# The greatest logit by a diagonal matmul and VectorE in place of GpSimd, and slots written as int32 at once

## The chip, the core and the metric

The kernel runs on one core of a Trainium2 chip. The core has five engines with queues of their own: TensorE (PE; its weight loads are shown as PEld), VectorE (DVE), ScalarE (ACT), GpSimd (POOL) and SyncE (SP, which here only issues transfers). They meet through semaphores. The metric is the device time of one execution in microseconds, as the median of several runs. The median before is 712.11 us, of three runs from 708.58 to 715.13.

## The reference

Eight sequences of 576 tokens go through an attention of eight heads with 64 columns each. Four heads see a local band of 32 keys, four see every 32nd key. The result, 4608 tokens by 512, goes through a mixture of eight experts with a capacity of 576 tokens each. Which expert takes which token is decided greedily over all pairs of token and expert:

```python
cap = N // E
logits = x @ w_gate
order = np.argsort(-logits.flatten())
for idx in order:                       # greatest logit first
    tok, e = (int(idx) // E, int(idx) % E)
    if assigned[tok] >= 0 or counts[e] >= cap:
        continue
    assigned[tok] = e
    counts[e] += 1
...
for e in range(E):
    mask = assigned == e
    h = np.maximum(x[mask] @ w1[e], 0.0)
    out[mask] = h @ w2[e]
```

## The kernel before, in words

**Attention and logits.** The first part runs over the eight sequences and the two kinds of heads, writes the tokens to device memory (`x_scr`, float16 in a high and a low part) and leaves the logits in `L`, 128 partitions by 36 columns by 8 experts: token 128c + p is partition p of column c. As columns are completed, VectorE keeps per partition the greatest absolute logit (`peak`, L521) and per token the greatest logit, its expert and a one-hot of it (`rm0`, `wm0`, `oh0`, by `point`, L192 to L196).

**The first expert's search.** The greedy rule is carried out expert by expert. The one whose capacity fills first is found by bisection over the logit at which it fills. The bisection needs a range that is the same on all partitions: `pk` (L715) is the greatest of `peak` per partition, `rng` (L717) the greatest of these over all partitions, present in each of them, and L718 keeps its power of two. L722 scales a constant grid of thresholds by it. `search0` (L768) then takes six rounds. In each, VectorE compares all tokens with 32 thresholds (`cm`, L778), TensorE counts per threshold and expert (L782), VectorE tests the counts against the capacity (L794), TensorE spreads the result over the partitions (L799), and VectorE forms the next thresholds (L802). The last round gives the expert, whose number `ei` (L887) lets SyncE fetch its weights (L987).

**Slots and indices.** `slots` (L890) numbers the expert's tokens by a prefix sum. `slot` (L918) holds 36 numbers per partition, from 0 to 575 for tokens taken and 8192 and more for others. `take` (L931) reads it to remove the tokens taken from the logits. `indices` (L937) turns it into a list of tokens: `si` splits a slot into its upper part (by 6 bits) and its lower 6 bits (L941 to L943), `sh` is the same in float16 (L945), one-hots of both parts (L947, L955, L949) go through a matmul (L963), and `idx` (L975) is the list. With it GpSimd's queue gathers the tokens (`xg`, L1072). The first expert's tokens are turned by TensorE (L1060), the others' by transposing transfers (L1075).

**Experts.** Each of the eight phases runs the two matrix products of one expert (L1159; L1207 and, for the last half tile, L1201), whose float32 weights are split on the chip into float16 high and low parts (L1020, L1021). Beside the matmuls of one phase run the search for the next expert (`search`, L816, comparison in L824, count in L840), its slots and indices, and the preparation of its weights.

**What sets the order.** TensorE's queue is written out by hand: a small planner in the kernel (due times in `chains`, a clock advanced by the cost of each matmul, L1259 to L1263) inserts the steps of the search among the matmuls; in the first phase ScalarE's queue is written out as well. The other engines' queues after the first search are ordered by the tile framework's list scheduler from its own cost estimates and the priorities of `urgent` (L744), so that one instruction less can exchange its neighbours. Semaphore waits follow from data and from buffers coming free. `rt` keeps two buffers of each name, `ps_r` two PSUM banks for all tiles named `pr_`.

Of the kernel before, what the change touches and what calls it, by code (L numbers as in the profile page):

```python
# [8 lines left out]
F32 = mybir.dt.float32  # L9
F16 = mybir.dt.float16  # L10
BF16 = mybir.dt.bfloat16
I32 = mybir.dt.int32
AF = mybir.ActivationFunctionType
OP = mybir.AluOpType
AX = mybir.AxisListType
# [25 lines left out]
TP = 128  # L41
NC = N // TP
DC, FC = DM // 128, FF // 128
NT = (CAP + 127) // 128
SLO = 64
# [87 lines left out]
def band_stride_attention_then_capacity_moe(ctx, tc, qt, kl, ks, nl, ns, wg, w1, w2, cst, out, dbg=None):  # L133
    nc = tc.nc
# [10 lines left out]
    ident = load_const("ident", [128, 128], F32)  # L145
# [30 lines left out]
    ones_f = const.tile([128, 128], F32, name="ones_f")  # L176
# [526 lines left out]
    rt = ctx.enter_context(tc.tile_pool(name="rt", bufs=2))  # L703
# [5 lines left out]
    ps_r = ctx.enter_context(tc.tile_pool(name="ps_r", bufs=2, space=PSUM))  # L709
# [4 lines left out]
    pk = rt.tile([128, 1], F32, name="pk")  # L714
    nc.vector.tensor_reduce(pk, peak, axis=AX.X, op=OP.max)  # L715
    rng = rt.tile([128, 1], F32, name="rng")
    nc.gpsimd.partition_all_reduce(rng, pk, 128, bass.bass_isa.ReduceOp.max)  # L717
    nc.vector.tensor_single_scalar(rng.bitcast(I32), rng.bitcast(I32), EXPM, op=OP.bitwise_and)  # L718
    grid = r1.tile([128, R0, J0 + 1], F32, name="grid")

# [169 lines left out]
    def slots(ph, rm, ohc, wmc, code, mv):  # L890
# [15 lines left out]
        with urgent(ph):  # L906
            pp = ps_r.tile([128, 512], F32, name="pr_")
            for j in range(2):
                nc.tensor.matmul(pp[:TP, j * 2 * NC:(j + 1) * 2 * NC], tri[:, j * TP:(j + 1) * TP], scf,
                                 start=(j == 0), stop=(j == 1), skip_group_check=True)  # L910
            off = rt.tile([TP, 2 * NC], F32, name="off")
            nc.vector.tensor_scalar(off, scf, -8192.0, 8192.0, op0=OP.mult, op1=OP.add)
            nc.vector.tensor_tensor_scan(inc[:, 1:], ones_f[:TP, :2 * NC], pp[:TP, 2 * NC:4 * NC], 0.0, op0=OP.mult,
                                         op1=OP.add)
            nc.vector.tensor_tensor(off, off, pp[:TP, :2 * NC], op=OP.add)
            nc.vector.tensor_tensor(off, off, inc[:, :2 * NC], op=OP.add)
            slot = rt.tile([TP, NC], F32, name="slot")
            nc.vector.tensor_tensor(slot, off[:, :NC], off[:, NC:], op=OP.min)  # L918
        return slot

# [16 lines left out]
    def indices(ph, slot):  # L937
        hurry = ph in HURRY
        with urgent(ph) if hurry else nullcontext():
            si = rt.tile([TP, 2, NC], I32, name="si")  # L940
            nc.vector.tensor_copy(si[:, 0], slot)  # L941
            nc.vector.tensor_single_scalar(si[:, 1], si[:, 0], SLO - 1, op=OP.bitwise_and)
            nc.vector.tensor_single_scalar(si[:, 0], si[:, 0], 6, op=OP.logical_shift_right)  # L943
            sh = rt.tile([TP, 2, NC], F16, name="sh")
            nc.vector.tensor_copy(sh, si)  # L945
            ohh = rt.tile([TP, SHI, NC], F16, name="ohh")
            nc.vector.tensor_tensor(ohh, sh[:, 0:1].to_broadcast([TP, SHI, NC]), iota[:, :SHI], op=OP.is_equal)  # L947
            rv = rvb[ph % 2]
            nc.vector.tensor_tensor(rv[:, :3 * SHI].rearrange("p (h a) c -> p h a c", a=3), ohh[:, :, None].to_broadcast([TP, SHI, 3, NC]),  # L949
                                    val[:, None].to_broadcast([TP, SHI, 3, NC]), op=OP.mult)  # L950
            nh = NC // 3
            ohl = []
            for h in range(3):
                o = r1.tile([TP, SLO, nh], F16, name=f"ohl{h}")
                nc.vector.tensor_tensor(o, sh[:, 1:2, h * nh:h * nh + nh].to_broadcast([TP, SLO, nh]),  # L955
                                        iota[:, :, :nh], op=OP.is_equal)
                ohl.append(o)
# [373 lines left out]
```

## Time and profile before

| | us |
|---|---|
| median of the runs | 712.11 (708.58 to 715.13) |
| profiled execution, its time | 713.84 |
| its span, first to last instruction | 712.1 |
| TensorE busy | 614.3 (86%) |
| VectorE busy | 465.3 (65%) |
| ScalarE busy | 318.9 (45%) |
| GpSimd busy | 156.7 (22%) |
| mean granted TensorE clock | 0.907 |

The profile is of one execution. Times in its rows are microseconds from the start of the span. A timeline row gives start, length, engine, line and instruction, output and inputs, and in brackets how long the engine had been idle and which event ended that. "issue" stands where no such event is seen. Rows that the profile merges carry a count (x16). The granted clock is the share of its full clock that TensorE was given. Attention ends near 220 us, the search of the first expert goes to about 243 us, the first expert's matmuls begin near 259 us, and the last transfer is issued after 701 us.

### The profile page before, as it was taken

The numbers are of one execution on the slowest core, as the hardware profiler recorded it, in microseconds if no ns is written. First come the engines' busy times: TensorE is split into PE (matmuls) and PEld (weight loads), VectorE is DVE, ScalarE is ACT, GpSimd is POOL, SyncE is SP. The second block draws the span as 40 slices with busy tenths as digits, with TensorE's granted clock in tenths as the row PEclk, the third lists the DMA queues.
The fourth block names the chain that finished last, engine by engine and source line by source line (L and its number), as shares of the span: only waits on it lengthen the run. The fifth ranks groups of instructions, "written<-read, shape, count | busy, mean of one in ns | idle before, by whom it ended". The sixth has DMA issues, their size and how long they took to land.

```text
span 712.1 us, 19031 instructions
## 1 busy us (share of the span) xinstructions
PE 614.3 (86%) x7974; PEld 392.3 (55%) x7977; DVE 465.3 (65%) x1326; ACT 318.9 (45%) x497; POOL 156.7 (22%) x152
## 2 busy tenths in 40 slices
PE   7778777788984368899989999999999989999993
PEld 4555555566663346546635745745654754755741
DVE  4797656787786788858857877867768543552200
ACT  3635634554521055555544644833823746452210
POOL 2053413323331030050041031211212111402011
PEclk9888978987786579999999999999999999999997
DMA  9999999999642270391671671852652684341010
GB/s 252 265 262 255 248 230 255 239 234 209 167 103 67 68 231 28 135 267 36 237 156 45 238 154 46 276 110 90 229 112 75 237 236 151 90 94 52 2 37 29
DMA packets 111472, 111.24 MB, mean 156 GB/s; under 512 B 76405, under 2 KB 84175, under 8 KB 110876
## 3 DMA queue, kind: packets, MB, share of 16 engines
q1 hardware_dynamic: 103307, 88.49, 47.9%
q0 software_dynamic: 7360, 21.15, 9.5%
q8 instruction: 62, 1.02, 0.6%
q10 hardware_dynamic: 720, 0.39, 0.2%
q14 instruction: 23, 0.18, 0.1%
HBM read 73.63 MB, written 18.87 MB: 130 GB/s over the span
## 4 chain that ended last, share of the span: by engine, by line
PE 26%; issue 12%; DVE 10%; DMA 8%; ACT 3%; POOL 2%; SPq 1%; POOLq 0%; ACTq 0%
PE ph L1207 12%; PE ph L1159 8%; DMA w<-in_w_dram 7%; PE ph L1201 2%; DVE w2l L1021 2%; ACT jk L1002 2%; DVE cm L824 1%; POOL out_dram L1218 1%; DVE hl L1167 1%; SPq L987 1%; DVE w1l L1021 1%; DMA xg<-x_scr,idx 1%; POOL xg L1072 1%; ACT hh L1166 1%; DVE ohl L955 1%
## 5 line engine op out<-in xcount | busy, mean ns | idle before, releaser
L1159 PE MATMUL ph<-xt,w1h 128*128 128x288 f16 (+2 forms) x1024 | 177.5, 287 | 2.0 <-ACT xt L1062 2.0
L1159 PEld LDWEIGHTS <-w1h 128*128 128x128 f16 x1024 | 97.4, 98 | 30.9 <-issue 5.3
L1159 PE MATMUL ph<-xt,w1l 128*128 128x288 f16 (+2 forms) x512 | 111.4, 287 | 0.0
L1218 POOL DMA_INDIRECT out_dram<-y,idx x40 | 44.0, 1100 | 254.4 <-ACT y L1217 229.1
L1207 PE MATMUL ph<-w2l,hh 128*128 128x512 f16 x256 | 97.8, 382 | 2.3 <-DVE w2l L1021 2.3
L1207 PE MATMUL ph<-w2h,hh 128*128 128x512 f16 x256 | 97.9, 382 | 1.9 <-ACT hh L1166 1.9
L1002 ACT ACTIVATE jk<-w 128x1024 f16<-128x1024 f32 x64 | 67.4, 1053 | 71.3 <-DMA w<-in_w_dram 69.8
L1207 PE MATMUL ph<-w2h,hl 128*128 128x512 f16 x256 | 97.8, 382 | 0.2 <-DVE hl L1167 0.2
L1167 DVE SCALAR_TENSOR_TENSOR hl<-ph,hh 128x576 f16<-128x576 f32 (+2 forms) x72 | 49.3, 686 | 53.6 <-ACT hh L1166 53.4
L1207 PEld LDWEIGHTS <-hh 128*128 128x128 f16 x512 | 47.9, 98 | 56.6 <-issue 5.1
L1166 ACT ACTIVATE hh<-ph 128x576 f16<-128x576 f32 (+2 forms) x72 | 42.5, 591 | 79.8 <-PE ph L1159 78.4
L1072 POOL DMA_INDIRECT xg<-x_scr,idx x40 | 43.2, 1080 | 135.5 <-DVE idx L975 100.5
L380 ACT ACTIVATE pr<-spa 128x576 f32<-128x576 f32 x32 | 20.8, 649 | 92.8 <-PE spa L376 83.3
L1217 ACT ACTIVATE y<-ph,so 128x512 f32<-128x512 f32 x32 | 21.9, 685 | 89.5 <-PE ph L1207 79.9
L1159 PEld LDWEIGHTS <-w1l 128*128 128x128 f16 x512 | 49.5, 98 | 14.1 <-issue 2.3
L428 POOL TENSOR_TENSOR xos<-xs,xos 118x768 f16<-118x768 f32 x16 | 27.1, 1694 | 113.4 <-ACT xos L427 113.4
L1021 DVE SCALAR_TENSOR_TENSOR w1l<-w,w_sw,w1h 128x512 f16<-128x512 f32 x64 | 46.1, 743 | 2.4 <-ACT w1h L1020 1.6
L1021 DVE SCALAR_TENSOR_TENSOR w2l<-w,w_sw,w2h 128x512 f16<-128x512 f32 x64 | 45.8, 743 | 1.7 <-ACT w2h L1020 1.6
L397 PE MATMUL po<-v_s,pr 64*54 64x65 f32 (+1 forms) x768 | 41.3, 259 | 5.3 <-issue 3.8
L1020 ACT ACTIVATE w1h<-w,w_sw 128x512 f16<-128x512 f32 x64 | 41.6, 711 | 8.4 <-DVE g L856 3.7
L1020 ACT ACTIVATE w2h<-w,w_sw 128x512 f16<-128x512 f32 x64 | 41.0, 710 | 5.0 <-DVE w_sw L208 4.9
L1207 PEld LDWEIGHTS <-hl 128*128 128x128 f16 x256 | 25.1, 98 | 30.2 <-issue 3.1
(571 smaller groups left out, 947.2 us busy)
## 6 DMA issues: line engine op xcount, KB each, us to landing
w<-in_w_dram SPq DMA_DIRECT2D x64, 512.0 KB
kl<-in_kl_dram SPq DMA_DIRECT2D x16, 304.0 KB
v_s<-in_ns_dram SPq DMA_DIRECT2D x16, 292.5 KB
v_l<-in_nl_dram SPq DMA_DIRECT2D x16, 292.5 KB
ks<-in_ks_dram SPq DMA_DIRECT2D x16, 288.0 KB
qs<-in_qt_dram SPq DMA_DIRECT2D x16, 288.0 KB
ql<-in_qt_dram SPq DMA_DIRECT2D x16, 288.0 KB
x_scr<-xol SPq DMA_DIRECT2D x8, 512.0 KB
```

The lines of the kernel that those rows point to most:

```text
L397: nc.tensor.matmul(po[r:r + n, j - j0], pr[k, o:o + n], u.vn[k, t, 2 * p + h], start=(j == j0), stop=(j == j1 - 1), skip_group_check=True)
L428: eng.tensor_tensor(u.xo[:nr, :, 1, c], xf, u.xo[:nr, :, 0, c], op=OP.subtract)
L1002: nc.scalar.activation(jk, wf[:, c * n4:(c + 1) * n4].rearrange("p c f -> p (c f)"), AF.Square, scale=1.41422, accum_out=sq[:, c:c + 1])
L1020: nc.scalar.activation(hi[:, c, f], wf[:, c, f], AF.Copy, scale=s_)
L1021: nc.vector.scalar_tensor_tensor(lo[:, c, f], wf[:, c, f], s_, hi[:, c, f], op0=OP.mult, op1=OP.subtract)
L1072: nc.gpsimd.indirect_dma_start(out=xg[:n], out_offset=None, in_=x_rows, in_offset=bass.IndirectOffsetOnAxis(ap=idx[:n, t:t + 1], axis=0))
L1159: nc.tensor.matmul(tile_[:, j, :w], wt[:, d, f * 128:(f + 1) * 128], xt[:, d // 2, xx, d % 2, c], start=(k == 0), stop=(k == 3 * DC - 1))
L1166: nc.scalar.activation(hv, src, AF.Relu)
L1167: nc.vector.scalar_tensor_tensor(lv, src, 0.0, hv, op0=OP.max, op1=OP.subtract)
L1207: nc.tensor.matmul(py, a[:, f, ts_], w[:, f], start=(k == 0), stop=(k == len(todo) - 1))
L1217: nc.scalar.activation(y, py, AF.Copy, scale=so[:, t:t + 1])
L1218: st = nc.gpsimd.indirect_dma_start(out=out_rows, out_offset=bass.IndirectOffsetOnAxis(ap=idx[:n, t:t + 1], axis=0), in_=y[:n], in_offset= ...
```

## The change

`rng` is no longer computed by GpSimd's reduction over partitions. VectorE multiplies the 128x128 identity by `pk`, so that `pkd` has the 128 values of `pk` on its diagonal. TensorE multiplies it with a matrix of ones into a PSUM tile of the pool `ps_r`, which puts all 128 values into each partition. VectorE takes the greatest of them along the free dimension.

`slot` becomes an int32 tile. The instruction of L918 writes it as such, `si` needs no conversion, and both of its halves are formed from `slot` directly. `take` reads the int32 tile, too.

```diff
@@ -714,7 +714,11 @@
     pk = rt.tile([128, 1], F32, name="pk")
     nc.vector.tensor_reduce(pk, peak, axis=AX.X, op=OP.max)
     rng = rt.tile([128, 1], F32, name="rng")
-    nc.gpsimd.partition_all_reduce(rng, pk, 128, bass.bass_isa.ReduceOp.max)
+    pkd = rt.tile([128, 128], F32, name="pkd", bufs=1)
+    nc.vector.tensor_scalar(pkd, ident, pk, None, op0=OP.mult)
+    prg = ps_r.tile([128, 512], F32, name="pr_")
+    nc.tensor.matmul(prg[:, :128], ones_f, pkd, start=True, stop=True)
+    nc.vector.tensor_reduce(rng, prg[:, :128], axis=AX.X, op=OP.max)
     nc.vector.tensor_single_scalar(rng.bitcast(I32), rng.bitcast(I32), EXPM, op=OP.bitwise_and)
     grid = r1.tile([128, R0, J0 + 1], F32, name="grid")
 
@@ -914,7 +918,7 @@
                                          op1=OP.add)
             nc.vector.tensor_tensor(off, off, pp[:TP, :2 * NC], op=OP.add)
             nc.vector.tensor_tensor(off, off, inc[:, :2 * NC], op=OP.add)
-            slot = rt.tile([TP, NC], F32, name="slot")
+            slot = rt.tile([TP, NC], I32, name="slot")
             nc.vector.tensor_tensor(slot, off[:, :NC], off[:, NC:], op=OP.min)
         return slot
 
@@ -938,9 +942,8 @@
         hurry = ph in HURRY
         with urgent(ph) if hurry else nullcontext():
             si = rt.tile([TP, 2, NC], I32, name="si")
-            nc.vector.tensor_copy(si[:, 0], slot)
-            nc.vector.tensor_single_scalar(si[:, 1], si[:, 0], SLO - 1, op=OP.bitwise_and)
-            nc.vector.tensor_single_scalar(si[:, 0], si[:, 0], 6, op=OP.logical_shift_right)
+            nc.vector.tensor_single_scalar(si[:, 1], slot, SLO - 1, op=OP.bitwise_and)
+            nc.vector.tensor_single_scalar(si[:, 0], slot, 6, op=OP.logical_shift_right)
             sh = rt.tile([TP, 2, NC], F16, name="sh")
             nc.vector.tensor_copy(sh, si)
             ohh = rt.tile([TP, SHI, NC], F16, name="ohh")
```

In the changed kernel the lines from L718 of before on stand four further down, and those behind the last hunk three. VectorE's queue at the start of the first search, before (L715 is `pk`, L718 the masking of `rng`, L722 the grid, `oh` and `wm` the last tokens' one-hots):

```order
L715 TENSOR_REDUCE pk<-peak 128x1
L193 TENSOR_TENSOR oh_96<-L,rm_95 128x40
L194 TENSOR_TENSOR oh_96<-oh_96,desc8h 128x40
L195 TENSOR_REDUCE wm_97<-oh_96 128x5
L196 TENSOR_TENSOR oh_96<-oh_96,wm_97 128x40
L718 TENSOR_SCALAR rng<-rng 128x1
L722 TENSOR_SCALAR grid<-small,rng 128x33
```

The same place in the changed kernel (L718 is the multiply, L721 the reduction out of PSUM, L722 the masking, L726 the grid):

```order
L715 TENSOR_REDUCE pk<-peak 128x1
L193 TENSOR_TENSOR oh_96<-L,rm_95 128x40
L718 TENSOR_SCALAR pkd<-ident,pk 128x128
L194 TENSOR_TENSOR oh_96<-oh_96,desc8h 128x40
L195 TENSOR_REDUCE wm_97<-oh_96 128x5
L196 TENSOR_TENSOR oh_96<-oh_96,wm_97 128x40
L721 TENSOR_REDUCE rng<-pr__3709 128x1
L722 TENSOR_SCALAR rng<-rng 128x1
L726 TENSOR_SCALAR grid<-small,rng 128x33
```

The multiply has gone between L193 and L194, and the reduction stands where VectorE used to wait for GpSimd. TensorE's queue has one instruction more, the matmul, ahead of the first count. GpSimd's queue has lost the two instructions of L717, the reduction and the reconfiguration ahead of it, and is otherwise the same.

VectorE's queue in the first phase, where it makes the slots and indices of the second expert beside the third one's search, before (`si` L941 to L943, `sh` L945, `pen`, `rmn` and `L` by `take`, `cm` the comparison of the search, `ohh`, `ohl`, `rv` the one-hots of the indices):

```order
L943 TENSOR_SCALAR si<-si 128x36
L934 TENSOR_TENSOR rmn<-rmn,pen 128x36
L935 TENSOR_TENSOR L<-L,pen 128x288
L945 CAST sh<-si 128x72
L824 TENSOR_TENSOR cm<-rmn,cand_3712 128x1152
L947 TENSOR_TENSOR ohh<-sh,iota 128x324
L955 TENSOR_TENSOR ohl_4751<-sh,iota 128x768
L949 TENSOR_TENSOR rv_3714<-ohh,val 128x972
L955 TENSOR_TENSOR ohl_4753<-sh,iota 128x768
L955 TENSOR_TENSOR ohl_4755<-sh,iota 128x768
L1021 SCALAR_TENSOR_TENSOR w2l<-w_4063,w_sw_4066,w2h 128x512
```

The same stretch in the changed kernel (`sh` is L948, `ohh` L950, `ohl` L958, `rv` L952, `rmn` L938, `cm` L828, `L` L939, the split of the weights L1024):

```order
L948 CAST sh<-si 128x72
L937 TENSOR_SCALAR pen<-slot 128x36
L196 TENSOR_TENSOR ohn<-ohn,wmn 128x288
L950 TENSOR_TENSOR ohh<-sh,iota 128x324
L958 TENSOR_TENSOR ohl_4753<-sh,iota 128x768
L952 TENSOR_TENSOR rv_3718<-ohh,val 128x972
L958 TENSOR_TENSOR ohl_4755<-sh,iota 128x768
L938 TENSOR_TENSOR rmn<-rmn,pen 128x36
L958 TENSOR_TENSOR ohl_4757<-sh,iota 128x768
L828 TENSOR_TENSOR cm<-rmn,cand_3716 128x1152
L939 TENSOR_TENSOR L<-L,pen 128x288
L1024 SCALAR_TENSOR_TENSOR w2l<-w_4067,w_sw_4070,w2h 128x512
```

Before, the comparison `cm` and the two steps of `take` ahead of it stood in front of the one-hots; now they stand behind all or most of them. The weight split follows the same work in both, less one instruction, as the conversion is gone. In the later phases the moves are smaller: `si` is finished two instructions earlier, and a neighbour or two of the one-hots changes places. TensorE's order is otherwise unchanged.

## The prediction

> **What bounds the kernel now.** I read the page first, for the span and the chain that ended last, then the busy time by stretches around the place of the change, then the timeline there. The first two lines below are the page's. The others are windows: start and end, length, then busy time and instructions of PE, PEld, DVE, ACT and POOL, the granted clock, the DMA share and GB/s.
>
> ```profile
> span 712.1 us, 19031 instructions
> ...
> PE 26%; issue 12%; DVE 10%; DMA 8%; ACT 3%; POOL 2%; SPq 1%; POOLq 0%; ACTq 0%
> ...
> 220.00:225.00 5.00, 0.00 (x0) 0.00 (x0) 1.81 (x10) 0.00 (x0) 0.00 (x0) 0.50 0.36 118
> ...
> 500.00:560.00 60.00, 56.95 (x447) 34.55 (x445) 41.62 (x131) 30.41 (x51) 11.91 (x10) 1.00 0.53 167
> ```
>
> Two regimes. From the first expert on, TensorE is the bound: 56.95 of 60 us busy in the stretch shown. Between attention (ended by 220 us) and the first expert there is one serial path, on which in five microseconds TensorE, ScalarE and GpSimd did nothing and VectorE worked 1.81 us. What is taken from that path moves everything behind it. The timeline shows who holds it (start, length, engine, line, instruction; in brackets the idle time ahead of it and its releaser); the first row is line 717 by source, from GpSimd's queue.
>
> ```profile
> L717 POOLq MODIFY_POOL_CONFIG  x2: 11/14/16, 219.3 to 219.3; - x2
> ...
> 221.06 0.16 DVE L715 TENSOR_REDUCE pk<-peak 128x1 f32<-128x5 f32 x1
> 221.14 0.19 DVE L193 TENSOR_TENSOR oh<-L,rm 128x40 f16<-128x40 f32 x1
> 221.37 0.18 DVE L194 TENSOR_TENSOR oh<-oh,desc8h 128x40 f16<-128x40 f16 x1
> ...
> 221.81 0.20 DVE L196 TENSOR_TENSOR oh<-oh,wm 128x40 f16<-128x40 f16 x1
> ...
> 225.14 0.38 POOL L717 PARTITION_ALL_REDUCE rng<-pk  x1 [6.08 <-issue]
> 225.56 0.15 DVE L718 TENSOR_SCALAR rng<-rng 128x1 int32<-128x1 int32 x1 [3.55 <-POOL rng L717]
> 225.75 0.24 DVE L722 TENSOR_SCALAR grid<-small,rng 128x33 f32<-128x33 f32 x1
> ```
>
> `pk` was there at 221.22 and VectorE was free at 222.01, but the reduction on GpSimd began at 225.14, held by nothing that the profile shows except the reconfiguration of GpSimd issued at 219.3: 5.84 us from one to the other, for an instruction of 0.38. VectorE waited 3.55 us, and the whole search of the first expert behind it.
>
> **The change, part one: the greatest value.** GpSimd's instruction and its reconfiguration go. In come a VectorE multiply of 128x128, a float32 matmul with 128 columns, and a VectorE reduction of 128 values out of PSUM. None is in the trace in that form; these are the nearest rows (the first two by source line, the others from the timeline).
>
> ```profile
> L291 PE MATMUL spb<-vsq,twos x16: 251/312/373, 22.4 to 191.9; 128*128 128x2 f32 x16
> ...
> L481 PE MATMUL po<-ident,xl x2: 272/300/328, 215.3 to 215.5; 128*128 128x128 f32 x2
> ...
> 220.76 0.19 DVE L521 TENSOR_REDUCE peak<-L 128x1 f32<-128x40 f32 x1
> ...
> 227.44 0.30 DVE L722 TENSOR_SCALAR grid<-small,rng 128x165 f32<-128x165 f32 x1
> ...
> 228.47 0.07 DVE L794 DVE_READ_ACCUMULATOR g<-pr__3719 32x1 f16 x1
> 228.60 0.16 PE L799 MATMUL pr__3770<-ih,ones_j 32*128 32x1 f16 x1 [0.65 <-DVE g L794]
> 228.80 0.26 DVE L802 SCALAR_TENSOR_TENSOR nx<-grid,pr__3770,pre 128x32 f32<-128x32 f32 x1 [0.25 <-PE pr__3770 L799]
> ...
> 250.76 0.45 DVE L192 TENSOR_REDUCE rmn<-L 128x36 f32<-128x288 f32 x1
> ```
>
> The multiply: 0.24 us for 33 columns and 0.30 for 165 in the same kind of instruction give 0.28 for 128. It stands right behind L193, so it runs from 221.37 to 221.65 and pushes L194 to L196 back by about 0.31: they end at 222.32 in place of 222.01. Hand-over from VectorE to TensorE took 0.06 (228.54 to 228.60), back 0.04 (228.76 to 228.80). The matmul can start at 221.71. The float32 rows say 0.25 to 0.37 at mixed clocks and 0.27 to 0.33 with 128 columns; at the half clock of this stretch I take up to twice 0.30, so it ends by 222.31. That is while VectorE is still in L196: **the matmul costs nothing, hidden behind L194 to L196**. Without that cover it would cost up to 0.6, and were it as long as 0.9, 0.3 of it would stick out. The reduction follows at 222.36; between 0.19 for 40 values and 0.45 for 288 lies 0.28 for 128, so it ends at 222.64, the masking (0.15, with gaps of 0.04) at 222.83, and the grid starts at 222.87 in place of 225.75: **2.88 us earlier**. Bounds: 2.6 with the long matmul, 3.0 with the reduction at its shortest row.
>
> The row prices GpSimd at 5.84 us, of which 3.55 stick out. The Trainium skill (GPSIMD Engine Reference, section 4.1, Engine selection) speaks against the change: reductions across partitions belong on GPSIMD and not on VectorE. The trace agrees only as far as the instruction itself goes, 0.38 us against my 1.27 from multiply to reduction.
>
> **Part two: slots as int32.** The conversion falls away; the instruction that made the slot and the two that read it keep their sizes.
>
> ```profile
> 245.27 0.18 DVE L941 CAST si<-slot 128x36 int32<-128x36 f32 x1
> 245.49 0.18 DVE L942 TENSOR_SCALAR si<-si 128x36 int32<-128x36 int32 x1
> ...
> 250.00 0.17 DVE L975 TENSOR_SCALAR idx<-idx 128x5 int32<-128x5 int32 x1
> ...
> 250.83 1.19 POOL L1072 DMA_INDIRECT xg<-x_scr,idx  x1 [25.31 <-issue]
> ...
> 254.44 1.02 PE L1105 MATMUL ph<-warm_i 128*128 128x512 bf16 x4
> ...
> 255.67 1.56 PE L1060 MATMUL ph<-ident_h,xg 128*128 128x128 f16 x16 [0.20 <-DMA xg<-x_scr,idx]
> ...
> 258.12 1.02 ACT L1062 ACTIVATE xt<-ph 128x1024 f16<-128x1024 f16 x1 [0.78 <-PE ph L1060]
> ...
> 259.19 0.59 PE L1159 MATMUL ph<-xt,w1h 128*128 128x256 f16 x2 [1.97 <-ACT xt L1062]
> ```
>
> From one row to the next 0.22 us, on the path to `idx`, none on the path to `ei`. A converting write and a read of int32 both cost 0.18 here already, so I see no price on the other side; bound 0.18 to 0.22. So the weights are asked for 2.88 us earlier and the gather 3.10. The two meet at the transposes of 255.67: TensorE, fed by the weights' path, had ended its filler matmuls at 255.46, and the gather landed 0.21 later. Shifted, they stand at 252.58 and 252.57. The gather's lead of 0.22 is just used up, and the first expert's matmuls follow about **3.0** earlier.
>
> In the later phases the same conversion goes seven more times, beside a busy TensorE. What of it can show is TensorE's waiting for the index matmuls' inputs (waits: engine, line, whom it waited for, total, times, longest):
>
> ```profile
> PE pr__7585 L963 <- DVE rv L949: 0.9, 1, 0.9
> ...
> PE pr__5527 L963 <- DVE ohl L955: 0.7, 1, 0.7
> ...
> PE pr__6884 L963 <- DVE ohl L955: 0.6, 1, 0.6
> ```
>
> Three phases, each shortened by at most 0.22, are 0.7; since VectorE's queue puts other work into most of those gaps, I take 0.2. The sum is 3.0 + 0.2 = **3.2 us**, between 2.6 and 3.9 (3.0 and 0.22 with all of the 0.7).
>
> The first phase has a move with a price. The second search's comparison (L824) now stands behind the index work instead of ahead of it.
>
> ```profile
> 295.54 0.44 DVE L935 TENSOR_TENSOR L<-L,pen 128x288 f32<-128x288 f32 x1
> ...
> 296.02 1.34 DVE L824 TENSOR_TENSOR cm<-rmn,cand 128x1152 f16<-128x1152 f32 x1
> 297.29 0.31 DVE L947 TENSOR_TENSOR ohh<-sh,iota 128x324 f16<-128x324 f16 x1
> ...
> 299.50 0.73 DVE L1021 SCALAR_TENSOR_TENSOR w2l<-w,w_sw,w2h 128x512 f16<-128x512 f32 x1
> ...
> 300.29 0.50 PE L1207 MATMUL ph<-w2l,hh 128*128 128x512 f16 x1 [2.28 <-DVE w2l L1021]
> ...
> 301.01 0.45 PE L840 MATMUL pr__4808<-ohn,cm 128*128 128x32 f16 x9
> ```
>
> From L947 to the weight split stand 2.21 us of index work; less 0.44 for the addition to `L` (L935), which moves behind it, the comparison ends 1.8 later, near 299.2. TensorE takes it up only at 301.01, because it waits for the split until 300.29, and the split stays where it was. Cost zero; the cover is 1.8 us.
>
> **The rivals.** *Slower: the gather has to load its code.* Until now the reconfiguration of 219.3 preceded the first gather; now only the first one, at the start, does. If the gather needs what the removed one brought, it pays those 5.84 us after `idx`, at 247.07, and starts at 252.9; before it was 250.83. The path is then 2.1 longer than before; with the 0.2 of the later phases 714.0. It decides from a load of more than 3.8 us on. For it: the first gather started 0.66 after `idx`. Against it: the removed load stands under line 717, and nothing is added ahead of the gather. The Trainium skill (GPSIMD Engine Reference, section 2.1, Instruction dispatch) has the first call of freshly loaded code pay some 6 us; the 5.84 here agrees. Chance 0.05.
>
> *The clock eats it, or doubles it.*
>
> ```profile
> 252.00:253.00 1.00, 0.42 (x1) 0.00 (x0) 0.93 (x3) 0.85 (x2) 0.70 (x2) 0.69 1.10 356
> 256.00:257.00 1.00, 1.00 (x13) 0.96 (x10) 1.00 (x2) 1.00 (x3) 0.92 (x1) 0.52 0.75 221
> 262.00:263.00 1.00, 1.00 (x11) 0.94 (x10) 0.71 (x3) 0.58 (x2) 0.00 (x0) 0.57 0.86 127
> ```
>
> Read as a switch between 0.5 and 1, the clock rose at 252.62, fell at 256.04 and rose at 262.86. So the first expert ran from 259.19 to 262.86 at half clock, which cost 1.8. Shifted work may meet the switch elsewhere: without that stretch it is 707.1; with another 6.8 us of it, 3.4 lost, 712.3. Steps of 3.42 and 6.82 us agree with the free-running window of 3.4 us that the Trainium skill (TensorE: Matmul & The Clock Gate, Part 1) gives. Chances 0.08 and 0.12.
>
> *The comparison's cover fails*: 1.8 given back, 710.7; 0.06. *The change does not do what it says*: were the 3.55 us not the reconfiguration's, only 0.38 would be saved for 1.27 added, 713.0; the row at 219.3 speaks against it; 0.03.
>
> **How the numbers follow.** The forecast has 0.66. The profiled execution took 713.84 (1.74 around its span) and would take 710.6; the median of the runs shown is 712.11, so 708.9. The runs shown lie from 3.5 under to 3.0 over their median. A new median may be some 2 off, which with the bounds of 2.6 to 3.9 gives 706 to 711.5 for the likeliest case alone. Taking in both clock cases, the comparison and most of the rest gives 705 to 713. One per cent is 7.1 us, about what a measurement here can tell from no change; no case reaches it by itself. Only the runs' spread on top of 3.2 does: faster 0.12, slower 0.03, within it 0.85.
>
> **What would show it.** The changed profile should have no reconfiguration near 219 us, a matmul of 0.3 to 0.6 us near 221.7, VectorE's wait ahead of the new reduction under 0.1, the first grid near 222.9, the first gather near 247.7, and TensorE's first expert near 256.2. I am wrong if a wait of a microsecond or more stands ahead of the new reduction or the first gather, or if the first expert starts early and the end does not follow.

## The result, and the profile after

The changed kernel took 709.77 us (median of 12 runs, 704.97 to 713.73), the kernel before 715.06 (12 runs, 708.58 to 718.72). The ratio is 0.9932, with a 95% interval of 0.9903 to 0.9962: 4.9 us less, between 2.7 and 6.9. Ratios and intervals leave out the executions that took over 1.5% more than the fastest of their kernel, medians have all of them. The forecast was 708.9 by a sum of 3.2 us, within one per cent of before with a chance of 0.85; measured it is 0.7% less. The profiled execution took 704.97, with a span of 703.2.

The page of the changed kernel, its span and the shares of the chain that ended last:

```profile
span 703.2 us, 19029 instructions
...
PE 27%; issue 12%; DVE 11%; DMA 7%; ACT 3%; POOL 2%; SPq 1%; POOLq 0%; DVEq 0%; ACTq 0%
```

The chain has the same make-up as before. Attention ended 3.08 us later in this execution than in the one of before (`pk` at 224.30 in place of 221.22), which the change cannot have caused, since all of it lies behind. So I count every place from the end of `pk`. The timeline of the changed kernel, from `pk` to the first grid, at the slots, at the first gather and at the first expert's first matmul (start, length, engine, line, instruction; in brackets the idle time ahead and its releaser):

```profile
224.14 0.16 DVE L715 TENSOR_REDUCE pk<-peak 128x1 f32<-128x5 f32 x1
224.22 0.19 DVE L193 TENSOR_TENSOR oh<-L,rm 128x40 f16<-128x40 f32 x1
224.34 0.29 DVE L718 TENSOR_SCALAR pkd<-ident,pk 128x128 f32<-128x128 f32 x1
...
224.74 0.50 PEld L720 LDWEIGHTS pr__3709<-pkd,ones_f 128*128 128x128 f32 x2 [2.11 <-issue]
...
224.77 0.77 PE L720 MATMUL pr__3709<-pkd,ones_f 128*128 128x128 f32 x2 [2.05 <-DVE oh L194]
224.97 0.20 DVE L196 TENSOR_TENSOR oh<-oh,wm 128x40 f16<-128x40 f16 x1
225.57 0.29 DVE L721 TENSOR_REDUCE rng<-pr__3709 128x1 f32<-128x128 f32 x1 [0.40 <-PE pr__3709 L720]
225.90 0.15 DVE L722 TENSOR_SCALAR rng<-rng 128x1 int32<-128x1 int32 x1
226.09 0.24 DVE L726 TENSOR_SCALAR grid<-small,rng 128x33 f32<-128x33 f32 x1
...
245.54 0.18 DVE L945 TENSOR_SCALAR si<-slot 128x36 int32<-128x36 int32 x1
245.64 0.17 DVE L946 TENSOR_SCALAR si<-slot 128x36 int32<-128x36 int32 x1
...
249.92 0.17 DVE L978 TENSOR_SCALAR idx<-idx 128x5 int32<-128x5 int32 x1
...
250.75 1.05 POOL L1075 DMA_INDIRECT xg<-x_scr,idx  x1 [29.46 <-DVE L L932]
...
259.18 0.38 PE L1162 MATMUL ph<-xt,w1h 128*128 128x256 f16 x2 [1.11 <-ACT xt L1065]
```

The reconfiguration of GpSimd and its reduction are gone. The grid starts 1.79 us after `pk`, where it was 4.53. The float32 matmul is two records, 0.77 us together, and VectorE waits 0.40 for it. The two halves of `si` start 0.10 apart. The gather follows `idx` by 0.66 us, as before.

The same places in every profile that is read here, from each one's timeline, in us after the end of `pk`. "Rest" is the time from the first expert's first matmul to the end of the span. "Half clock" is the time in that rest, less its last 12 us, at which TensorE had only half its clock: twice the missing share of the granted clock, summed over stretches of 4 us. The kernels below the second row are those of the experiments.

| kernel | grid | expert `ei` | `idx` ends | first matmul | rest | half clock |
|---|---|---|---|---|---|---|
| before | 4.53 | 21.70 | 28.95 | 37.97 | 452.9 | 10.6 |
| after | 1.79 | 18.82 | 25.79 | 34.88 | 444.0 | 0.0 |
| both_again | 1.79 | 18.82 | 25.80 | 34.96 | 449.4 | 7.0 |
| heat12 | 1.78 | 18.81 | 25.78 | 34.74 | 449.6 | 6.8 |
| hurry07 | 1.79 | 18.82 | 25.79 | 34.76 | 454.1 | 6.8 |
| range_only | 1.79 | 18.83 | 26.15 | 35.13 | 459.2 | 23.8 |
| range_only_2 | 1.78 | 18.81 | 26.14 | 35.17 | 459.3 | 21.6 |
| slots_only | 4.31 | 21.49 | 28.41 | 37.66 | 453.1 | 11.0 |
| range_bf16 | 1.19 | 18.22 | 25.20 | 34.41 | 452.9 | 11.0 |
| early_load | 0.74 | 17.99 | 25.25 | 34.41 | 452.8 | 10.9 |
| all_reduce_twice | 4.04 | 21.21 | 28.45 | 36.89 | 452.9 | 10.9 |
| delay | 13.12 | 30.17 | 37.15 | 46.18 | 458.5 | 13.8 |
| bf16_hurry07 | 1.20 | 18.24 | 25.22 | 34.21 | 459.1 | 17.2 |

Up to the first matmul the changed kernel gains 3.09 us, and both profiles of it (after and `both_again`) agree within 0.1. Behind it the rest of this execution is 8.9 us shorter than that of before, which the change by itself does not explain. One place shows what differs. These are 4.5 us around the wait for the first weight split of the second matrix product, 41 us into the first expert, ahead of which TensorE sat idle for 2.28 us before and for 2.18 after. First the window of before, then that of after (start and end, length, busy time and instructions of PE, PEld, DVE, ACT, POOL, granted clock, DMA share, GB/s):

```profile
299.00:303.50 4.50, 3.21 (x53) 1.96 (x52) 1.80 (x6) 1.87 (x4) 1.04 (x1) 0.66 0.45 137
```

```profile
299.00:303.50 4.50, 4.29 (x68) 2.62 (x69) 1.86 (x13) 1.01 (x3) 1.99 (x2) 1.00 0.66 227
```

Behind the same wait the clock was halved in one execution and not in the other. In the profiled execution of the changed kernel this happened at no place of the rest, its last 12 us aside; in that of before it happened at three (0, 41 and 96 us behind the first matmul), for some 3.4 us each.

The traces show what differs. In each of the 13 profiles all changes of the granted clock lie on a grid of 3.413 us, to within 0.002 us. The two intervals of that grid around the wait, first in before, then in after:

```profile
297.00:300.41 3.41, 1.13 (x6) 0.47 (x5) 3.32 (x8) 2.37 (x5) 0.00 (x0) 1.00 0.25 103
300.41:303.83 3.42, 3.42 (x53) 1.86 (x51) 0.71 (x4) 0.69 (x1) 1.04 (x1) 0.50 0.69 220
```

```profile
295.39:298.80 3.41, 1.64 (x8) 0.65 (x7) 3.41 (x7) 2.32 (x5) 0.00 (x0) 1.00 0.46 187
298.80:302.21 3.41, 3.00 (x59) 2.11 (x60) 1.26 (x6) 1.21 (x3) 1.02 (x1) 1.00 0.51 163
```

In before the whole wait lies in one interval, in which TensorE was busy for 1.13 us, and the next interval is at half clock. In after a border of the grid, at 298.80, cuts the wait: TensorE was busy for 1.64 and 3.00 us, and the clock stayed. In the nine other profiles that have this wait it lies in one interval, with TensorE busy for 1.13 to 1.23 us, and half clock follows each time. In `both_again`, the same kernel as after, the grid lies otherwise against the wait, so the program alone does not set that.

### The profile page after: what moved, and what is told of

It reads as the page before. It is cut to its first block, busy times and chain, and to the rows that moved or that the text cites. A ratio compares the mean times of both kernels' runs of the same rounds, so it can differ in the third digit from the quotient of the medians.

```text
span 703.2 us, 19029 instructions
## 1 busy us (share of the span) xinstructions
PE 616.0 (88%) x7976; PEld 396.3 (56%) x7979; DVE 465.0 (66%) x1320; ACT 318.5 (45%) x497; POOL 155.6 (22%) x151
## 4 chain that ended last, share of the span: by engine, by line
PE 27%; issue 12%; DVE 11%; DMA 7%; ACT 3%; POOL 2%; SPq 1%; POOLq 0%; DVEq 0%; ACTq 0%
PE ph L1210 15%; PE ph L1162 6%; DMA w<-in_w_dram 6%; PE ph L1204 3%; DVE w1l L1024 2%; DVE hl L1170 2%; DVE cm L828 2%; ACT jk L1005 1%; DVE w2l L1024 1%; POOL out_dram L1221 1%; DMA xg<-x_scr,idx 1%; POOL xg L1075 1%; SPq L990 0%; ACT hh L1169 0%; ACT w2h L1023 0%
## 5 line engine op out<-in xcount | busy, mean ns | idle before, releaser
L428 POOL TENSOR_TENSOR xos<-xs,xos 118x768 f16<-118x768 f32 x16 | 26.8, 1680 | 117.7 <-ACT xos L427 117.7
L397 PE MATMUL po<-v_s,pr 64*54 64x65 f32 (+1 forms) x768 | 43.9, 272 | 6.1 <-ACT pr L380 3.7
L1024 DVE SCALAR_TENSOR_TENSOR w1l<-w,w_sw,w1h 128x512 f16<-128x512 f32 x64 | 46.0, 742 | 2.4 <-ACT w1h L1023 2.4
L1024 DVE SCALAR_TENSOR_TENSOR w2l<-w,w_sw,w2h 128x512 f16<-128x512 f32 x64 | 45.9, 744 | 1.7 <-ACT w2h L1023 1.6
```

The costliest lines, as they stand in the source:

```text
L397: nc.tensor.matmul(po[r:r + n, j - j0], pr[k, o:o + n], u.vn[k, t, 2 * p + h], start=(j == j0), stop=(j == j1 - 1), skip_group_check=True)
L428: eng.tensor_tensor(u.xo[:nr, :, 1, c], xf, u.xo[:nr, :, 0, c], op=OP.subtract)
L1024: nc.vector.scalar_tensor_tensor(lo[:, c, f], wf[:, c, f], s_, hi[:, c, f], op0=OP.mult, op1=OP.subtract)
```

## The experiments

Two theories stood at the start. By the first, the change is worth what it takes off the path to the first expert, about 3.1 us, and whatever goes beyond is the scatter of the rest. By the second, the new order makes the later phases faster as such, which would explain 4.9 us and a rest of 444.0. A third point was whether it is the reconfiguration that made GpSimd's reduction dear.

### Each part alone

`range_only` is the kernel before with the matmul in place of GpSimd's reduction, slots still float32:

```diff
-    nc.gpsimd.partition_all_reduce(rng, pk, 128, bass.bass_isa.ReduceOp.max)
+    pkd = rt.tile([128, 128], F32, name="pkd", bufs=1)
+    nc.vector.tensor_scalar(pkd, ident, pk, None, op0=OP.mult)
+    prg = ps_r.tile([128, 512], F32, name="pr_")
+    nc.tensor.matmul(prg[:, :128], ones_f, pkd, start=True, stop=True)
+    nc.vector.tensor_reduce(rng, prg[:, :128], axis=AX.X, op=OP.max)
```

> Part one alone: the range by matmul and VectorE, the slots as before in float32. Theory A (only the path from pk to the first expert counts, one for one): from the end of pk to the start of the grid 1.8 us as in the changed kernel (4.53 before), to the first expert's first matmul 35.2 us (37.97 before), the time 2.8 us under the kernel before. Theory B (the later phases, reordered by part two, gave the rest of the 5 us measured for the whole change): 2.8 as well, and the missing 2 us appear with the slots alone. Theory C (the later phases scatter from run to run): 2.8, and nothing but scatter with the slots alone.

`slots_only` is the kernel before with only the int32 slots:

```diff
-            slot = rt.tile([TP, NC], F32, name="slot")
+            slot = rt.tile([TP, NC], I32, name="slot")
...
-            nc.vector.tensor_copy(si[:, 0], slot)
-            nc.vector.tensor_single_scalar(si[:, 1], si[:, 0], SLO - 1, op=OP.bitwise_and)
-            nc.vector.tensor_single_scalar(si[:, 0], si[:, 0], 6, op=OP.logical_shift_right)
+            nc.vector.tensor_single_scalar(si[:, 1], slot, SLO - 1, op=OP.bitwise_and)
+            nc.vector.tensor_single_scalar(si[:, 0], slot, 6, op=OP.logical_shift_right)
```

> Part two alone: int32 slots, the range by GpSimd. Theory A: from the end of pk to the grid 4.5 us, to the list of indices 0.35 less than before (28.6 against 28.95), the time 0.3 to 0.6 us under the kernel before, which is within the measurement. Theory B: about 2 us under it, with the first phase's order of VectorE as in the changed kernel. Theory C: as A.

Measured on one chip, beside a before of 720.23: `range_only` 720.65, ratio 1.0005 (0.997 to 1.0041), and `slots_only` 719.01, ratio 0.9979 (0.9943 to 1.0015). The first number was a surprise, since its profile has the whole gain on the path: the first matmul stands at 35.13 in place of 37.97, 2.84 earlier. Its rest is 459.2, among the longest of the table, with the clock halved for 23.8 us. So the first part's gain was made and then lost behind the first expert in that execution.

Both agree on the worth of the slots. From `ei` to the end of `idx` it is 7.25 us before and 7.32 in `range_only`, 6.97 after and 6.92 in `slots_only`. Int32 slots take off 0.33 alone and 0.35 where they join the matmul; from before to after it is 0.28. The conversion's row in the timeline of `range_only`, with what stands around it, shows why it is more than one step:

```profile
241.86 0.18 DVE L945 CAST si<-slot 128x36 int32<-128x36 f32 x1
242.07 0.18 DVE L946 TENSOR_SCALAR si<-si 128x36 int32<-128x36 int32 x1
242.29 0.18 DVE L947 TENSOR_SCALAR si<-si 128x36 int32<-128x36 int32 x1
```

Here each of the three instructions works on the output of the one ahead or overwrites its input, and they start 0.21 and 0.22 apart. In the changed kernel the two halves of `si` both read `slot` and start 0.10 apart, so besides a step of 0.22 some 0.1 goes.

Since a second run was to show whether 1.0005 was the kernel's own, `range_only_2` is the same kernel on another chip.

> Part one alone once more, as its first result (no difference, 1.0005) lies at the edge of theory A's 2.8 us (0.996) although its profile had the path as expected and seven windows at half clock behind it. Theory C: the windows fall otherwise, the time is 1 to 4 us under the kernel before. If part one alone really loses in the later phases what it gains on the path: no difference again, and five or more windows at half clock behind the first expert's start.

It took 719.5 beside 720.32, ratio 0.9958 (0.9927 to 0.9989). The two results overlap between 0.997 and 0.9989. The path is the same to 0.04 us, and the rest is again 459.3 with the clock halved for 21.6 us. Whether this order of the later phases calls up more of these windows, or two profiles happened to fall alike, stays open. The second trace, with over 20 us at half clock, is what the expectation named as the sign of a loss; the second time is not, and it speaks against a fixed loss of 6 us.

### Is it the path? A delay put into it

`delay` is the changed kernel with the masking of `rng` repeated 60 times more, which changes nothing in its value:

```diff
     nc.vector.tensor_single_scalar(rng.bitcast(I32), rng.bitcast(I32), EXPM, op=OP.bitwise_and)
+    for _ in range(60):
+        nc.vector.tensor_single_scalar(rng.bitcast(I32), rng.bitcast(I32), EXPM, op=OP.bitwise_and)
```

> The changed kernel with 60 further maskings of rng in a row on VectorE, each waiting for the one before: 60 x 0.19 = 11.4 us more between pk and grid. Theory A: all of it reaches the end, some 8 us over the kernel before (11.4 less the change's 3.2; less 4.9 if its measured ratio is taken). Rival: the weights, transfers or the clock absorb part of it, and the end moves by less than 9 of the 11.4, 6 us or less over the kernel before.

The grid stands at 13.12 in place of 1.79, 11.33 later, the first matmul at 46.18, 11.3 later, and the time is 730.26, ratio 1.0128 (1.0051 to 1.0204): 9.2 us over before, between 3.7 and 14.7 by four runs. With 3.1 gained and 11.3 lost it should be 8.2. In the profile the whole delay reaches the first matmul, and the rest, 458.5, is longer than in the two profiles of the changed kernel, so there is no sign that any of the delay was made good there. The time fits that, but four runs do not rule out the rival of 6 us or less.

### The changed kernel again

`both_again` repeats the changed kernel without an edit.

> The changed kernel once more, beside the three below on one chip. Theory A with C (the path is 3.1 us shorter up to the first expert, and everything behind it scatters by whole clock windows of 3.4 us that fall differently in each execution): the profile gives 1.79 us from pk to the grid and about 34.9 to the first matmul; behind that 444 us plus some 2 to 3 us for each window at half clock; the time 2 to 5 us under the kernel before. Theory B (the changed kernel's later phases are faster as such): 444 us again from the first matmul to the end.

715.1 beside 716.87, ratio 0.9971 (0.9931 to 1.0012): 2.1 us less, between 4.9 less and 0.9 more. With the first result (2.7 to 6.9 less) both intervals hold the 3.1 us of the path, and neither needs more. The rest is 449.4 in this profile, 5.4 more than in the other execution of the same kernel. That alone takes away the reason for the second theory.

The rows of the table decide it. Where the clock was halved at three places, the rest is 452.8 to 453.1, and that is so in five profiles: before, `early_load` and `all_reduce_twice` with the old order of the later phases, `slots_only` and `range_bf16` with the new one. In `both_again` and `heat12` it was halved at two (0 and 41 us behind the first matmul), and the rest is 449.4 and 449.6; in the first profile of the changed kernel at none, 444.0. **The theory that the new order makes the later phases faster as such falls**: in these five profiles, with the clock halved equally often, both orders take the same time to 0.3 us. That the order changes how often the clock is halved is not ruled out: the five profiles with the old order have 10.6 to 23.8 us at half clock, the six with the new one 0 to 13.8 (the kernels with `hurry07`'s edit left aside). So few executions do not tell this from chance.

How much of the scatter the clock itself makes is not settled. In the rest, less its last 12 us, TensorE is busy for 417.7 us after, in as many instructions as its 428.0 in `range_only`. First the window of after, then that of `range_only`:

```profile
259.18:691.20 432.02, 417.70 (x3193) 251.97 (x3193) 275.56 (x787) 210.47 (x356) 81.04 (x74) 1.00 0.46 133
```

```profile
255.73:703.00 447.27, 428.01 (x3193) 255.20 (x3193) 278.03 (x794) 211.45 (x356) 79.89 (x74) 0.97 0.46 129
```

Of 15.2 us more, 10.3 are busy time and 4.9 idle. Nor does the half-clock time fix the rest: `delay` has 2.8 us more of it than `slots_only` and a rest 5.4 longer, and TensorE's idle times of over 0.1 us in the rest add up to 23.6 us there and to 19.2 in `slots_only`.

### Can the clock be held up?

`heat12` is the changed kernel with twelve filler matmuls in place of six ahead of the first expert.

```diff
-SCALE_AT, TURN_AT, TAKE_AT, SEARCH_AT, TURN_U, W_EARLY, WARM0, WARM1, TURNS, TURN_E = 7, 9, 9, 10, 0, 1, 6, 4, 3, 2
+SCALE_AT, TURN_AT, TAKE_AT, SEARCH_AT, TURN_U, W_EARLY, WARM0, WARM1, TURNS, TURN_E = 7, 9, 9, 10, 0, 1, 12, 4, 3, 2
```

> The changed kernel with 12 filler matmuls in place of 6 behind the list of indices (the filler's result is not used), so that TensorE is busy over the gap of 2 us ahead of the next four. If the first expert's cold start is a window in which TensorE was not busy enough, the clock stays at 1 up to and over the first matmuls; they ran at half clock for 3.5 to 4 us in four of the six profiles so far, at 1.8 us each, so on average 1 to 2 us under the changed kernel. If the window's state does not hang on the filler, no difference. If the filler stands in the way of the transposes, up to 0.5 us more from pk to the first matmul than 34.9.

715.04 beside 716.87, ratio 0.9973 (0.9937 to 1.0009), like `both_again` on the same chip. TensorE in its timeline, the fillers and the first expert:

```profile
249.06 4.17 PE L1108 MATMUL ph<-warm_i 128*128 128x512 bf16 x12
...
253.95 1.02 PE L1108 MATMUL ph<-warm_i 128*128 128x512 bf16 x4
...
258.50 0.38 PE L1162 MATMUL ph<-xt,w1h 128*128 128x256 f16 x2 [2.22 <-ACT xt L1065]
```

And its window behind that:

```profile
258.50:262.00 3.50, 3.50 (x29) 2.56 (x29) 3.12 (x9) 3.39 (x6) 0.00 (x0) 0.54 0.78 105
```

The first expert still began at about half clock. The fillers cover another gap than the one that counts: the 2.22 us in which TensorE waits for ScalarE's copy of the turned tokens lie behind them, in the interval from 255.36 to 258.78, in which TensorE was busy for 1.20 us; the next one is at half clock. That the halved stretches last some 3.4 us and that all changes lie on a grid of 3.413 us agrees with the Trainium skill (TensorE: Matmul & The Clock Gate, Part 1), where the clock is set by a free-running window of that length.

`hurry07` takes the second phase out of those that run their index work urgently, so that the wait at 41 us goes.

```diff
-HURRY = (0, 1, 7)
+HURRY = (0, 7)
```

> The changed kernel without the raised priority for the indices of the first phase: VectorE then takes the last weight split, the end of take and the comparison of the second search ahead of the one-hots. The changed order costs nothing by the prediction, as TensorE waits 2.2 us for that split anyway. Theory A: with the split one to three places earlier that wait shrinks by 0.7 to 2.2 us; what is late next is the index list of the second expert, by 2 to 3 us, which nobody waits for; the time 0 to 2 us under the changed kernel's. Theory B (the order in the first phase is where the gain of later phases came from): slower than the changed kernel by 2 us.

714.28 beside 716.87, ratio 0.9951 (0.9911 to 0.9991). The wait for the split is gone, but its waits show what came in its place (TensorE, line, whom it waited for, total, times, longest):

```profile
PE ph L1210 <- ACT hh L1169: 3.8, 1, 3.8
PE pr__4958 L853 <- DVE r L850: 2.6, 1, 2.6
...
PE pr__5528 L966 <- DVE ohl L958: 1.4, 1, 1.4
```

Against 1.9, nothing and 0.7 in the first profile of the changed kernel. The first of them is no sign of the edit, as it is 3.3 in `both_again`; the second stands in neither. So the 2.2 us won in one place are given back in another, and its rest of 454.1 is not shorter; in time it cannot be told from `both_again`.

### What makes GpSimd's reduction dear

`all_reduce_twice` is the kernel before with the reduction called a second time on the first one's result, which leaves the value as it is:

```diff
-    nc.gpsimd.partition_all_reduce(rng, pk, 128, bass.bass_isa.ReduceOp.max)
+    rn0 = rt.tile([128, 1], F32, name="rn0")
+    nc.gpsimd.partition_all_reduce(rn0, pk, 128, bass.bass_isa.ReduceOp.max)
+    nc.gpsimd.partition_all_reduce(rng, rn0, 128, bass.bass_isa.ReduceOp.max)
```

> The kernel before with a second reduction over all partitions behind the first on GpSimd, of the same value. If what was paid was the reconfiguration, the second one adds 0.4 to 0.7 us: pk to grid 5.0 to 5.2 in place of 4.53. If the reduction itself takes the 5.8 us, it adds about 6: some 10. One look; the time says nothing at that size in the first case.

One execution, 718.84 beside a median of 716.87. Its timeline at GpSimd:

```profile
222.87 1.39 POOL L428 TENSOR_TENSOR xol<-xl,xol 128x640 f16<-128x640 f32 x1 [3.67 <-ACT xol L427]
...
227.14 0.16 DVE L715 TENSOR_REDUCE pk<-peak 128x1 f32<-128x5 f32 x1
...
230.29 0.38 POOL L718 PARTITION_ALL_REDUCE rn<-pk  x1 [6.03 <-issue]
230.77 0.35 POOL L719 PARTITION_ALL_REDUCE rng<-rn  x1
```

From the end of the last subtraction (L428, 224.26) to the first reduction pass 6.03 us, 2.99 of them after `pk` was there (227.30). The second reduction starts 0.48 after the first. So the first call pays 6 us and the next one nothing of it. This agrees with the Trainium skill (GPSIMD Engine Reference, section 2.1, Instruction dispatch), which has the first call of freshly loaded code pay some 6 us.

The load starts when GpSimd is done with its last subtraction, so what sticks out behind `pk` depends on how long before the end of `pk` that was: 2.16 us before and 3.03 here, with the grid at 4.53 and at 4.04, although there is a reduction more (5.0 to 5.2 had been expected). The load itself varied less, from 5.88 us between subtraction and reduction in `slots_only` (grid at 4.31, again 2.16 ahead) to 6.08 before. In the 12 profiles that keep the subtraction on GpSimd the subtraction ends between 2.16 and 3.12 us ahead of the end of `pk`, at 2.16 or 2.17 in seven. So what the change takes off the path is not one number: the 3.1 us hold for an execution with the 2.16 us of the profile of before; with 3.12 it would be, by an estimate from these times, about 1 less.

`early_load` takes that subtraction, the last unit's second half, away from GpSimd, and is otherwise the kernel before:

```diff
-                at(2 * j + p if j else 2, lambda u=u, p=p: u.finish(p, nc.gpsimd))
+                at(2 * j + p if j else 2, lambda u=u, p=p: u.finish(p, nc.vector if u is todo[-1] and p else nc.gpsimd))
```

> The kernel before, with GpSimd's reduction kept, but its last elementwise subtraction (L428 of the last unit's second half) given to VectorE, so that GpSimd's reconfiguration can be issued some 5 us earlier. If the reconfiguration is all that made GpSimd slow, it is issued near 8 us ahead of pk and done before it: pk to grid 0.7 to 1.0 us in place of 4.53 (0.38 for the reduction, 0.15 for the masking and the hand-overs); VectorE pays up to 0.85 for the subtraction ahead of pk; the time 2.7 to 3.8 us under the kernel before, as good as the change without a matmul. If the reduction waits for something else, pk to grid stays over 3.

The medians are 720.34 and 720.32, the ratio is 0.9984 (0.9956 to 1.0012): between 3.2 us less and 0.9 more. Line 717 by source and then the timeline:

```profile
L717 POOLq MODIFY_POOL_CONFIG  x2: 1/1/1, 219.1 to 219.2; - x2
```

```profile
223.64 0.83 DVE L428 TENSOR_TENSOR xol<-xl,xol 128x640 f16<-128x640 f32 x1
...
225.70 0.16 DVE L715 TENSOR_REDUCE pk<-peak 128x1 f32<-128x5 f32 x1
...
226.00 0.38 POOL L717 PARTITION_ALL_REDUCE rng<-pk  x1 [7.08 <-DVE oh L193]
226.41 0.15 DVE L718 TENSOR_SCALAR rng<-rng 128x1 int32<-128x1 int32 x1 [0.41 <-POOL rng L717]
226.60 0.24 DVE L722 TENSOR_SCALAR grid<-small,rng 128x33 f32<-128x33 f32 x1
```

The reconfiguration is issued at 219.1, nearly 7 us ahead of `pk`, and now GpSimd waits for VectorE (`<-DVE oh L193`) and not the other way round. The grid stands 0.74 after `pk`: less than with the matmul, 1.79. **It is the reconfiguration that cost the time, not the reduction**, and moving it gains about as much on this path. The subtraction on VectorE lies ahead of `pk`, though, where it takes 0.75 (223.64 to the next instruction at 224.39), so 2.8 net of the 3.56 at the first matmul are left; the time does not show them beyond doubt.

### Narrower numbers for the same step

`range_bf16` is the changed kernel with the masking to a power of two ahead of the matmul, which then loses nothing in bfloat16:

```diff
+    nc.vector.tensor_single_scalar(pk.bitcast(I32), pk.bitcast(I32), EXPM, op=OP.bitwise_and)
-    pkd = rt.tile([128, 128], F32, name="pkd", bufs=1)
-    nc.vector.tensor_scalar(pkd, ident, pk, None, op0=OP.mult)
+    pkd = rt.tile([128, 128], BF16, name="pkd", bufs=1)
+    nc.vector.tensor_scalar(pkd, ident_b, pk, None, op0=OP.mult)
...
-    nc.tensor.matmul(prg[:, :128], ones_f, pkd, start=True, stop=True)
+    nc.tensor.matmul(prg[:, :128], ones_b, pkd, start=True, stop=True)
...
-    nc.vector.tensor_single_scalar(rng.bitcast(I32), rng.bitcast(I32), EXPM, op=OP.bitwise_and)
```

> The changed kernel with pk masked to its power of two first, then the multiply and the matmul in bfloat16 (a power of two is exact there), and no masking behind. If the 0.40 us that VectorE waited ahead of the reduction are the float32 matmul's (0.77 us with its two passes), the matmul takes some 0.2 to 0.3, the wait falls under 0.1, and pk to grid is 1.2 to 1.4 in place of 1.79; the time 0.5 us under the changed kernel's, not to be told by the time. If the wait is the hand-over between the engines, it stays near 0.4 and the path near 1.8.

716.61 beside 720.23, ratio 0.9952 (0.9921 to 0.9982). Its timeline:

```profile
222.47 0.16 DVE L715 TENSOR_REDUCE pk<-peak 128x1 f32<-128x5 f32 x1
...
223.17 0.29 PE L721 MATMUL pr__3710<-pkd,ones_b 128*128 128x128 bf16 x1 [2.50 <-DVE pkd L719]
223.25 0.20 DVE L196 TENSOR_TENSOR oh<-oh,wm 128x40 f16<-128x40 f16 x1
223.49 0.29 DVE L722 TENSOR_REDUCE rng<-pr__3710 128x1 f32<-128x128 f32 x1
223.82 0.24 DVE L726 TENSOR_SCALAR grid<-small,rng 128x33 f32<-128x33 f32 x1
```

The matmul is one record of 0.29 in place of two of 0.77, it ends together with L196, and VectorE no longer waits. The grid stands at 1.19, 0.6 earlier than in the changed kernel, and the first matmul at 34.41, 0.5 earlier. This is the form in which the matmul really is hidden.

`bf16_hurry07` joins this edit and that of `hurry07`.

> The range in bfloat16 and the first phase's indices without raised priority, together, as a version that may beat the change. pk to grid 1.19, to the first matmul 34.3 to 34.4; the time 3.5 to 5 us under the kernel before, 0.5 to 1.5 under the changed kernel, which the time can hardly tell.

716.8 beside 720.32, ratio 0.9908 (0.987 to 0.9946) from six of eight runs, the lowest ratio measured. Its interval overlaps those of `range_bf16`, `hurry07` and the changed kernel, so that it is better than these is not shown; on the path it has the same places, the grid at 1.20 and the first matmul at 34.21.

## Why the prediction was right, and where not

**From `pk` to the grid: 2.88 forecast, 2.74 measured; one term mis-sized.** The step "the matmul costs nothing, hidden behind L194 to L196" failed. The matmul was taken as 0.30 to 0.60 from float32 rows with few columns or at mixed clocks, and took 0.77 at the half clock, as two records with a weight load each. It started 0.14 behind the multiply and not 0.06. It ended at 225.54; L196 had ended at 225.17, and VectorE waited 0.40, not under 0.1. The rule that were it as long as 0.9, 0.3 would stick out, and the bound of 2.6, covered this. Part of the miss was given back because the multiply started 0.04 after `pk`, beside L193, and not 0.15 after. The reduction came as forecast, 0.29 for 0.28. From `pk` to the grid it is 4.53 by GpSimd before, 1.79 by the matmul, 1.19 by the one in bfloat16, and 0.74 by GpSimd in `early_load`, which pays 0.75 on VectorE for it. The rule of the Trainium skill (GPSIMD Engine Reference, section 4.1, Engine selection) that was weighed against the change, that reductions across partitions belong on GPSIMD, holds here only with the code loaded in time.

**The conversion: 0.22 forecast, 0.28 to 0.35 measured**, from `ei` to `idx`. The term counted the step that goes and missed that the two left no longer depend on each other.

**The gather, 3.10 forecast and 3.16 measured at `idx`; the first expert, 3.0 and 3.09.** These hold. Between the grid and `ei` lies a gain of 0.14 that I had not seen: 17.03 to 17.05 us with the matmul in every kernel, 17.17 to 17.25 with GpSimd's reduction. It is made in the first round, where the test of the counts starts 2.51 us behind the grid in place of 2.63; its cause stays open.

**The comparison moved behind the index work: nothing forecast, nothing found.** It ends ahead of the point where it is needed. The first phase of the changed kernel (`cm` the comparison, `w2l` the weight split):

```profile
296.78 1.34 DVE L828 TENSOR_TENSOR cm<-rmn,cand 128x1152 f16<-128x1152 f32 x1
...
298.42 0.73 DVE L1024 SCALAR_TENSOR_TENSOR w2l<-w,w_sw,w2h 128x512 f16<-128x512 f32 x1
...
299.20 0.38 PE L1210 MATMUL ph<-w2l,hh 128*128 128x512 f16 x1 [2.18 <-DVE w2l L1024]
...
299.63 0.38 PE L844 MATMUL pr__4810<-ohn,cm 128*128 128x32 f16 x9
```

It ended at 298.12, the count took it up at 299.63, and TensorE had waited for the split until 299.20, as before.

**The later phases: 0.2 forecast, none shown; mis-sized.** The waits for the index matmuls' inputs, which I took to shrink by up to 0.22 each, in the changed kernel:

```profile
PE pr__6206 L966 <- DVE rv L952: 0.9, 1, 0.9
PE pr__7583 L966 <- DVE rv L952: 0.7, 1, 0.7
...
PE pr__5528 L966 <- DVE ohl L958: 0.7, 1, 0.7
...
PE pr__6883 L966 <- DVE ohl L958: 0.4, 1, 0.4
```

Phase by phase, what was 0.9 before is 0.7 here (`pr__7583`), 0.6 is 0.4 (`pr__6883`), 0.7 stayed (`pr__5528`), and `pr__6206` waits 0.9 where it did not before. In the five profiles whose rest is 452.8 to 453.1 the idle times ahead of the index matmuls add up to 3.0 to 3.4 us with the old order and to 2.3 with the new one; but TensorE's idle times in the rest add up to 18.6 to 18.7 with the old and to 18.6 and 19.2 with the new. What is saved there is waited for elsewhere, and the rest is the same.

**The rivals.** The gather did not have to load code: it follows `idx` by 0.66 in both. The change did what it says, and the 3.55 us of waiting were the reconfiguration's (`all_reduce_twice`, `early_load`). The rival of the clock was right in what it names and wrong in where it puts it. Whether the first expert meets a half-clock stretch is not fixed by the change: two profiles of the changed kernel differ in it, one with the stretch, one without. The wait 41 us behind it points to what decides: in 11 profiles it is whether the wait falls into one interval of the clock's grid. With the waits that follow, this moves single executions by more than the change does.

**The time.** The sum was 3.2, the path gives 3.1; the ratios of two sets of runs give 4.9 (2.7 to 6.9) and 2.1 (0.9 more to 4.9 less). That 709.77 came so near 708.9 is luck: with more runs the kernel before stood at 715.06 and not at 712.11, 2.95 above the base of the sum, and the first set's medians lie 5.29 apart, 2.09 more than the sum. The two nearly cancel.

## What to carry to other kernels

Where an engine waits for "issue" ahead of a short instruction on GpSimd, look for a reconfiguration on its queue: the price is the load, and one can either replace the instruction or let the load start earlier, by ending the other kind of work on GpSimd sooner. A matmul meant to hide beside VectorE's work should be priced in its own type, since float32 came as two records and 0.77 us where bfloat16 took 0.29. Where executions scatter by more than an edit is worth, measure the edit from the point where it starts to the point where the path ends, and compare what follows only between profiles in which the clock was halved equally often, knowing that the clock is not all of the scatter.

## What was not expected of the hardware

The second of two reductions in a row on GpSimd started 0.48 us after the first, which had taken 6.03 us to start. Two VectorE instructions that read the same tile and do not depend on each other started 0.10 us apart, dependent ones of the same size 0.21 to 0.22. The same wait of TensorE of 2.2 us, at the same place of the program, was followed by some 3.4 us at half clock in ten executions, in which it lay in one interval of the clock's grid of 3.413 us, and by none in the one in which a border of the grid cut it. Profiles with none, two and three such stretches behind the first matmul have a rest of 444.0, 449.5 and 452.9 us (`hurry07`, in another order, has 454.1 with two).
